# A spectral-filter and SwiGLU block on one core: Strassen products for one more chunk, with the scaling of w_down by gb moved to GpSimd

## The chip, the cores and the metric

The kernel runs on one core of a Trainium2 chip. The metric is the device time of one execution in microseconds (us). In a fast run the time lies within 1.5% of the kernel's fastest. A ratio is the mean time of one kernel's fast runs over the mean of the other's from the same rounds, with a 95% interval, so it is not quite the ratio of the medians that are quoted beside it. Below 0.98 counts as faster, above 1.02 as slower.

Engine names in the profile: PE is TensorE (matmul), PEld its weight loads, DVE is VectorE, ACT is ScalarE, POOL is GpSimd.

## The reference

```python
mod = (silu(c) @ w_mod).reshape(1, 6, 1, -1)           # sa, ca, ga, sb, cb, gb
h = layernorm(x) * (1 + ca) + sa                       # x: 2048 x 640, bf16
x = x + ga * irfft2(rfft2(h) * (w_r + 1j * w_i))       # spectral filter
h = layernorm(x) * (1 + cb) + sb
x = x + gb * ((silu(h @ w_gate) * (h @ w_up)) @ w_down)   # 640 -> 1728 -> 640
```

The change touches the last two lines, and the end of the third, with which they overlap.

## The kernel before

The 2048 rows are 16 tiles of 128. The last step of the spectral filter, called **phase 3** here, makes one tile after the other: TensorE multiplies, VectorE adds the residual from PSUM. Meanwhile the second layer norm of the first tiles starts: squares on ScalarE, variance on VectorE, the power -1/2 on GpSimd, normalization on VectorE, a transposing DMA, and the modulation (1 + cb, sb) in place, which is called "mod" below.

The feed-forward part then runs in five chunks of 2, 4, 4, 4 and 2 tiles. Each chunk has a gate/up stage (called C0 to C4) and a down stage (D0 to D4). In C0 and C1 gate/up is plain: 5 products for each of the 26 outputs. From C2 on it is a Strassen form: 7 block products in place of 8, for which sums of weight blocks (`GS`, `UG`) are needed once. The kernel before makes those sums in C1 on VectorE. It also scales the 14 row blocks of w_down by gb (`wd_fold`) on VectorE, five in phase 3 and nine in C0.

```python
def ln2_mod(ci):
    h2T = h2T_of(ci)
    for c5 in range(NC5):
        if ci == 0:
            nc.gpsimd.tensor_scalar(h2T[:, :, c5, :], h2T[:, :, c5, :], one_p_cb[:, c5:c5 + 1], modcols[:, 2, c5:c5 + 1],
                                    ALU.mult, ALU.add)
        elif c5 % 2 == 0 or ci > 1:
            nc.vector.tensor_scalar(...)          # the same operands
        else:
            nc.scalar.activation(...)
...
def gu_table(i, q):                                # weight sums, 256 columns at a time
    fs = slice(256 * q, 256 * q + 256)
    tt = nc.vector.tensor_tensor
    up1, up2, ga1, ga2 = (gu_w(u, k)[:, :, fs] for u in (1, 0) for k in range(2))
    s1, s2, s3, s4 = (g[:, :, fs] for g in GS)
    if i == 0:
        tt(s1, ga1, ga2, ALU.add)
    elif i == 1:
        tt(s2, s1, up1, ALU.subtract)
    elif i == 2:
        tt(s3, up1, ga1, ALU.subtract)
    elif i == 3:
        tt(s4, up2, s2, ALU.subtract)
    else:
        tt(UG[:, fs], Wgu[:, 1, 4, fs], Wgu[:, 0, 4, fs], ALU.subtract)

def wd_fold(f2):
    nc.vector.tensor_tensor(Wd_sb[:, f2, :], Wd_sb[:, f2, :], gb_bc[:], ALU.mult)
...
for t in range(NT):                                # phase 3
    ...                                            # six matmuls into PSUM
    nc.vector.scalar_tensor_tensor(x1[:, t, :]..., ops..., 1.0, x_sb[:, t, :]..., ALU.mult, ALU.add, accum_out=st2[:, t, 0:1])
    ...
    if 4 <= t <= 5:
        ln2_xn(0, t - 4)                           # normalization
    if t == 5:
        ln2_tr(0)                                  # transposing DMA
        load_gu(1024, 1664)
    ...
    if t == 10:
        ln2_mod(0)
    if t >= 7 and t % 2:
        wd_fold((13, 0, 1, 2, 3)[(t - 7) // 2])
...
for ci, (t0, n) in enumerate(chunks):
    if ci >= 2:
        gate_up_pairs(ci, ATc)                     # Strassen
    else:
        for fc in range(NFC - 1):                  # 13 column blocks
            half(0)                                # 5 matmuls, Silu on ScalarE
            half(1)                                # 5 matmuls, product on VectorE
            if ci == 0:
                if fc < 9:
                    wd_fold(fc + 4)
                ...                                # squares, variance; ln2_xn for chunk 1
                if fc == 10:
                    wd_rest()                      # copies of w_down's last row block
            else:
                for q in (2 * fc, 2 * fc + 1):
                    if q < 24:
                        gu_table(q % 4, q // 4)
                if fc % 2 == 1:
                    gu_table(4, fc // 2)
                ...
```

## Time and profile before

| | before |
|---|---|
| median of 3 runs | 259.76 us (258.53 to 259.96) |
| profiled span, mean granted clock | 258.0 us, 0.992 |
| TensorE, VectorE, ScalarE, GpSimd busy | 96%, 78%, 58%, 27% |

From the chain of waits of the kernel before, in order of time: start, length, engine and line, number of instructions.

```profile
87.62 14.19 PE psum L1015 x130
...
110.44 28.06 PE psum L1015 x130
```

L1015 is the plain gate/up, first C0, then C1. With the five matmuls at 109.36 that the fence leaves out, C1 takes 109.36 to 138.50, 29.14 us, and C2, in the Strassen form with as many tiles, follows the same chain from 152.24 to about 179, 26.8 us. That difference is what the change wants.

The same kernel by windows (from : to, length, busy time with number of instructions of PE, PEld, DVE, ACT and POOL, granted clock, DMA share, GB/s), one for C0, one for C1, one for C2:

```profile
87.10:101.80 14.70, 14.70 (x137) 12.99 (x137) 13.72 (x42) 8.14 (x23) 2.02 (x2) 1.00 0.25 49
109.40:138.50 29.10, 29.10 (x137) 13.07 (x135) 25.94 (x66) 15.59 (x31) 1.32 (x1) 1.00 0.02 6
152.20:179.00 26.80, 26.80 (x234) 22.41 (x231) 20.21 (x46) 18.30 (x34) 0.00 (x0) 1.00 0.06 17
```

TensorE has no gap in any of them. In C0 VectorE is busy for 13.72 of 14.70 us.

GpSimd in the kernel before, from its timeline (start, length, line, operation, out and in with shapes, count, idle time before it):

```profile
81.08 3.24 POOL L767 TENSOR_SCALAR rW<-rW,one_p_cb,modcols 128x256 bf16<-128x256 bf16 x5 [5.51 <-DMA rW<-rL]
90.72 1.01 POOL L741 TENSOR_TENSOR rstd_1286<-rstd_1286,mhalf 128x4 f32<-128x4 f32 x1 [6.40 <-DVE rstd_1286 L737]
```

Around the end of phase 3 GpSimd does five mods for chunk 0 (L767) and a variance power (L741), and little else. It looks free. While it does the mods, VectorE does two folds, in 0.49 and 0.57 us; the other folds take 0.48 or 0.49.

### The profile page before, as it was taken

The numbers are of one execution on the slowest core, as the hardware profiler recorded it, in microseconds if no ns is written. First come the engines' busy times: TensorE is split into PE (matmuls) and PEld (weight loads), VectorE is DVE, ScalarE is ACT, GpSimd is POOL, SyncE is SP. The second block draws the span as 40 slices with busy tenths as digits, with TensorE's granted clock in tenths as the row PEclk, the third lists the DMA queues.
The fourth block names the chain that finished last, engine by engine and source line by source line (L and its number), as shares of the span: only waits on it lengthen the run. The fifth ranks groups of instructions, "written<-read, shape, count | busy, mean of one in ns | idle before, by whom it ended". The sixth has DMA issues, their size and how long they took to land.

```text
span 258.0 us, 6291 instructions
## 1 busy us (share of the span) xinstructions
PE 248.6 (96%) x2423; PEld 191.8 (74%) x2423; DVE 202.3 (78%) x529; ACT 150.9 (58%) x280; POOL 69.3 (27%) x121
## 2 busy tenths in 40 slices
PE   7999997999999999999999999999999999999994
PEld 3778866899789888744445678886678887669963
DVE  2599788998889897499886966788875878875682
ACT  3578756998678664028652367765256676225740
POOL 4277772577214011000020450000450000440012
PEclk9799999999999999999999999999999999999999
DMA  7989999999998205100003211000412000211001
GB/s 233 392 249 303 290 404 198 174 387 381 316 307 211 102 5 104 41 14 9 0 3 71 70 42 36 3 0 12 94 51 64 0 0 4 51 53 56 3 3 51
DMA packets 44923, 30.84 MB, mean 120 GB/s; under 512 B 21599, under 2 KB 43102, under 8 KB 44510
## 3 DMA queue, kind: packets, MB, share of 16 engines
q1 hardware_dynamic: 44748, 30.23, 40.8%
q8 instruction: 19, 0.31, 0.5%
q10 hardware_dynamic: 146, 0.21, 0.3%
q14 instruction: 10, 0.08, 0.1%
HBM read 22.87 MB, written 4.72 MB: 107 GB/s over the span
## 4 chain that ended last, share of the span: by engine, by line
PE 74%; DVE 5%; ACT 2%; issue 2%; POOL 1%; POOLq 0%; ACTq 0%; DVEq 0%
PE psum L1041 22%; PE psum L1015 18%; PE psum L928 16%; PE psum L913 3%; PE psum L649 3%; PE psum L586 2%; PE psum L550 2%; PE psum L812 2%; PE psum L994 2%; PE psum L815 2%; DVE rM L573 1%; PE psum L607 1%; PE psum L638 1%; PE psum L654 1%; ACT rE L622 1%
## 5 line engine op out<-in xcount | busy, mean ns | idle before, releaser
L1015 PE MATMUL psum<-rW 128*128 128x512 bf16 (+1 forms) x290 | 49.0, 328 | 0.0
L1015 PEld LDWEIGHTS <-rW 128*128 128x128 bf16 x290 | 28.3, 98 | 18.4
L1041 PEld LDWEIGHTS <-rW 128*128 128x128 bf16 (+1 forms) x396 | 34.1, 98 | 3.6
L1041 PE MATMUL psum<-rW 128*128 128x256 bf16 (+1 forms) x252 | 35.3, 255 | 0.0
L953 POOL TENSOR_TENSOR rM<-rM,rL 128x320 f32<-128x320 f32 x7 | 7.8, 1117 | 100.5 <-ACT rL L949 100.5
L928 PEld LDWEIGHTS <-rX 128*128 128x128 bf16 (+1 forms) x175 | 15.8, 97 | 8.8 <-issue 1.8
L573 DVE TENSOR_TENSOR rM<-psum,rW 128x384 bf16<-128x384 f32 (+2 forms) x42 | 20.5, 542 | 1.4 <-PE psum L550 1.1
L928 PEld LDWEIGHTS <-rE 128*128 128x128 f16 x168 | 16.4, 98 | 6.9 <-DVE rE L885 0.6
L899 DVE TENSOR_TENSOR rA<-psum,rM 128x320 bf16<-128x320 f32 x25 | 11.6, 484 | 12.0 <-POOL rM L957 5.8
L928 PE MATMUL psum<-rE 128*128 128x320 f16 x126 | 20.6, 299 | 0.3 <-DVE rE L885 0.3
L1018 ACT ACTIVATE rX<-psum 128x256 f32<-128x256 f32 (+1 forms) x26 | 12.7, 487 | 13.0 <-PE psum L1015 12.2
L1041 PE MATMUL psum<-rE,rW 128*128 128x256 f16 (+1 forms) x144 | 19.9, 255 | 0.0
L928 PE MATMUL psum<-rA,rX 128*128 128x320 bf16 (+1 forms) x119 | 19.5, 301 | 0.1
L741 POOL TENSOR_TENSOR rstd_1286<-rstd_1286,mhalf 128x4 f32<-128x4 f32 (+2 forms) x4 | 4.0, 1010 | 51.4 <-DVE rstd_1286 L737 51.4
L1021 DVE TENSOR_TENSOR rX<-psum,rX 128x256 bf16<-128x256 f32 (+1 forms) x26 | 14.4, 557 | 2.6 <-PE psum L1015 2.3
L389 DVE SCALAR_TENSOR_TENSOR rE<-rE,mv,psum 128x648 bf16<-128x648 f32 (+1 forms) x17 | 14.1, 841 | 2.4 <-PE psum L322 2.1
L342 ACT COPY rE<-psum 128x640 bf16<-128x640 bf16 x16 | 11.1, 691 | 6.7 <-PE psum L340 6.7
L817 DVE SCALAR_TENSOR_TENSOR rM<-psum,rX 128x640 f32<-128x640 f32 x16 | 13.1, 821 | 2.1 <-PE psum L815 2.1
L1091 DVE TENSOR_TENSOR rX<-rH,rL 128x512 bf16<-128x512 bf16 x15 | 6.4, 425 | 10.3 <-ACT rL L1089 10.3
L589 ACT CAST rY<-psum 128x512 bf16<-128x512 f32 (+2 forms) x21 | 12.2, 589 | 3.8 <-PE psum L586 3.7
L1041 PEld LDWEIGHTS <-rE 128*128 128x128 f16 x144 | 12.7, 98 | 1.5
L657 ACT CAST rL<-psum 128x640 bf16<-128x640 f32 x16 | 10.9, 689 | 4.0 <-PE psum L654 3.0
(198 smaller groups left out, 622.0 us busy)
## 6 DMA issues: line engine op xcount, KB each, us to landing
out_dram<-rA SPq DMA_DIRECT2D x32, 80.0 KB, 1.6
rM<-in_w_mod_dram SPq DMA_DIRECT2D x3, 800.0 KB, 9.4
rA<-in_B_w_down_dram SPq DMA_DIRECT2D x1, 2080.0 KB, 17.3
rX<-in_A_x_dram SPq DMA_DIRECT2D x3, 640.0 KB, 9.6
rM<-in_w_mod_dram SPq DMA_DIRECT2D x1, 1600.0 KB, 7.4
rW<-in_B_w_gate_dram SPq DMA_DIRECT2D x2, 640.0 KB, 7.0
rW<-in_B_w_up_dram SPq DMA_DIRECT2D x2, 640.0 KB, 8.2
rW<-in_A_w_i_dram SPq DMA_DIRECT2D x1, 1024.0 KB, 11.0
```

The costliest lines, as they stand in the source:

```text
L342: nc.scalar.copy(hT[:, :, 0:128], _rev(xt, 127, [[128, NC5], [-1, 128]]) if flipped(t) else xt)
L389: nc.vector.scalar_tensor_tensor(Zv[:, h], Cv[:, h], mv[:, t, 0:1], zps[:, h], ALU.mult, ALU.subtract)
L573: nc.vector.tensor_tensor(PP[:, 1:4, hl], xv[:, :, hl], in1, ALU.mult)
L589: nc.scalar.copy(Y2[:, 0:n, :], yps[:, 0:n, :])
L657: nc.scalar.copy(VT[:], vps[:, 0:5, :])
L817: nc.vector.scalar_tensor_tensor(x1[:, t, :].rearrange("p (m r) -> p m r", r=4), ops.rearrange("p r m -> p m r"), 1.0, x_sb[:, t, :].rearr ...
L899: nc.vector.tensor_tensor(xo, src, x1[:, t, lo:lo + 320], ALU.add)
L928: nc.tensor.matmul(o, lhsT=lhsT, rhs=rhs, start=start, stop=stop, skip_group_check=True)
L1015: nc.tensor.matmul(gu[u], lhsT=Wgu[:, u, c5, ff * 128:(ff + 1) * 128], rhs=h2T[:, :, c5, :], start=(c5 == 0), stop=(c5 == NC5 - 1))
L1018: nc.scalar.activation(sg[:, 0:N], gu[0], ACT.Silu)
L1021: nc.vector.tensor_tensor(ATc[:, ff, :], gu[1], sg[:, 0:N], ALU.mult)
L1041: nc.tensor.matmul(o[:, f], lhsT=w, rhs=b, start=(start and f == 0 and i == 0), stop=(stop and f == F - 1 and i == len(ops) - 1), skip_gro ...
```

## The change

Its intent: run C1 in the Strassen form as well. The weight sums must then exist before C1, so they move into C0. To make room on VectorE, the 14 folds go to GpSimd, the first sum (S1) is made by two DMAs that GpSimd issues (one converts gate's upper half to fp16, the second adds the lower half), chunk 1's normalization goes to ScalarE, and the mods for chunk 0 go from GpSimd to VectorE, one a tile.

```diff
-    def ln2_mod(ci):
+    def ln2_mod(ci, cs=range(NC5)):
-        for c5 in range(NC5):
-            if ci == 0:
-                nc.gpsimd.tensor_scalar(...)
-            elif c5 % 2 == 0 or ci > 1:
+        for c5 in cs:
+            if c5 % 2 == 0 or ci != 1:
                 nc.vector.tensor_scalar(...)
@@
     def gu_table(i, q):
-        fs = slice(256 * q, 256 * q + 256)
+        fs = slice(512 * q, 512 * q + 512)
@@
     def wd_fold(f2):
-        nc.vector.tensor_tensor(Wd_sb[:, f2, :], Wd_sb[:, f2, :], gb_bc[:], ALU.mult)
+        nc.gpsimd.tensor_tensor(Wd_sb[:, f2, :], Wd_sb[:, f2, :], gb_bc[:], ALU.mult)
+    def gu_dma(k):
+        w = B_w_gate[256 * k:256 * k + 256, 0:1536].rearrange("(c5 dp) f -> dp c5 f", dp=P)
+        nc.gpsimd.dma_start(GS[0][:], w, accum_op=ALU.add if k else ALU.bypass)
@@ before phase 3
+        gu_dma(0)
@@ phase 3, after tile t
+            if t == 8:
+                gu_dma(1)
-            if t == 10:
-                ln2_mod(0)
-            if t >= 7 and t % 2:
-                wd_fold((13, 0, 1, 2, 3)[(t - 7) // 2])
+            if 10 <= t <= 14:
+                ln2_mod(0, (t - 10,))
+            if t == 14:
+                ln2_var(2, 4)
+                ln2_pow(2, 4)
+            for q in range(max(t - 4, 0), min(t - 3, 9)) if t < 14 else range(9, 14) if t == 15 else ():
+                wd_fold((13, 0, 6, 1, 7, 2, 8, 3, 9, 4, 10, 5, 11, 12)[q])
@@ chunks
-        if ci >= 2:
-            gate_up_pairs(ci, ATc)
+        if ci:
+            gate_up_pairs(ci, ATc, [...normalization of chunk 2 and five wd_tables... if ci == 1 else []])
         else:
+            tables = [lambda i=i, q=q: gu_table(i, q) for q in range(3) for i in range(1, 5)]
             for fc in range(NFC - 1):
@@
-                    if fc < 9:
-                        wd_fold(fc + 4)
-                    if 3 <= fc <= 6:
-                        ln2_xn(1, fc - 3)
+                for _ in range(2 if fc < 8 else 1):
+                    if tables:
+                        tables.pop(0)()
+                if 1 <= fc <= 4:
+                    ln2_xn_act(1, fc - 1)
... (squares rearranged; chunk 1's input sums made in D0, five of the eight down tables moved
     from D0 to C1; the last tiles' variance and power moved from C1 to the start of D1;
     the whole plain form of chunk 1 removed)
```

Nine folds stand in phase 3 on GpSimd, five more behind the power that C1's normalization needs.

More of the change, by code (lines that the diff above doesn't have):

```diff
@@ L761, in ln2_tr @@
             xn2c[:, 0:n].rearrange("p tl (c q) -> p (tl c) q", c=NC5))
-    def ln2_mod(ci):
+    def ln2_mod(ci, cs=range(NC5)):
         h2T = h2T_of(ci)
-        for c5 in range(NC5):
-            if ci == 0:
-                nc.gpsimd.tensor_scalar(h2T[:, :, c5, :], h2T[:, :, c5, :], one_p_cb[:, c5:c5 + 1], modcols[:, 2, c5:c5 + 1],
-                                        ALU.mult, ALU.add)
-            elif c5 % 2 == 0 or ci > 1:
+        for c5 in cs:
+            if c5 % 2 == 0 or ci != 1:
                 nc.vector.tensor_scalar(h2T[:, :, c5, :], h2T[:, :, c5, :], one_p_cb[:, c5:c5 + 1], modcols[:, 2, c5:c5 + 1],
@@ L917, in down_plain @@
                 ln2_mod(1)
-        for i in range(4):
+                h_sums(1)
+        for i in range(3):
             wd_tables(i, 0)
-            wd_tables(i, 1)
     def down_pair(ATc, t, j, nxt):
@@ L1022, in gu_plain, with gate_up_pairs @@
         return half
-    def gate_up_pairs(ci, ATc):
+    def gate_up_pairs(ci, ATc, extra):
         n = chunks[ci][1]
@@ L1110, in gate_up_pairs @@
             step(7, p - 2)
+            if p and extra:
+                extra.pop(0)()
             if n == 2:
@@ L1149, in adaln_block_kernel @@
         ATc = AT[:, 0:NFC * N].rearrange("p (f q) -> p f q", f=NFC)
-        if ci >= 2:
-            gate_up_pairs(ci, ATc)
+        if ci:
+            gate_up_pairs(ci, ATc, [lambda i=i: (ln2_xn_act(2, i), wd_tables(i, 1)) for i in range(4)] + [lambda: wd_tables(3, 0)] if ci == 1 else [])
         else:
             fin13 = gu13(ci, ATc)
+            tables = [lambda i=i, q=q: gu_table(i, q) for q in range(3) for i in range(1, 5)]
             for fc in range(NFC - 1):
@@ L1160, in adaln_block_kernel @@
                     fin13()
-                if ci == 0:
-                    if fc < 9:
-                        wd_fold(fc + 4)
-                    if fc in (0, 2, 4, 6):
-                        ln2_sq(6 + fc // 2)
-                    if fc == 0:
-                        ln2_var(2, 4)
-                        ln2_pow(2, 4)
-                    if 3 <= fc <= 6:
-                        ln2_xn(1, fc - 3)
-                    if fc == 6:
-                        ln2_tr(1)
-                    if fc == 8:
-                        ln2_var(6, 4)
-                        ln2_pow(6, 4)
-                    if fc == 10:
-                        ln2_nb(6, 4)
-                        wd_rest()
-                else:
-                    for q in (2 * fc, 2 * fc + 1):
-                        if q < 24:
-                            gu_table(q % 4, q // 4)
-                    if fc % 2 == 1:
-                        gu_table(4, fc // 2)
-                    if fc in (4, 8, 12):
-                        for i in range(4):
-                            a_sum(ATc, 0, i, slice(fc // 2 - 2, fc // 2))
-                    if fc < 6:
-                        ln2_sq(10 + fc)
-                    if fc == 7:
-                        ln2_var(10, 6)
-                        ln2_pow(10, 6)
-                    if fc == 10:
-                        ln2_nb(10, 6)
-                    if 6 <= fc <= 9:
-                        ln2_xn_act(2, fc - 6)
+                if fc == 0:
+                    ln2_nb(2, 4)
+                if fc == 8:
+                    ln2_var(6, 4)
+                    ln2_pow(6, 4)
+                if fc == 10:
+                    ln2_nb(6, 4)
+                    wd_rest()
+                for _ in range(2 if fc < 8 else 1):
[3 more added lines that the diff above has]
+                    ln2_xn_act(1, fc - 1)
+                if fc == 4:
+                    ln2_tr(1)
+                if fc in (0, 5, 6, 7, 8, 9, 10, 12):
+                    ln2_sq({0: 6}.get(fc, fc + 2 if fc < 12 else 13))
+            ln2_sq(14)
+            ln2_sq(15)
         if ci == 0:
@@ L1200, in adaln_block_kernel @@
         if ci == 1:
-            a_sum(ATc, 0, 4)
+            ln2_var(10, 6)
+            ln2_pow(10, 6)
+            ln2_nb(10, 6)
         if ci + 1 < len(chunks):
```

## The prediction

> **What bounds it.** TensorE: the page gives it 96% of a 258.0 us span, and the chain of waits is 74% TensorE matmuls, almost unbroken from the first gate/up (87.1 us) to 243 us. By stretch of that chain: chunk 1 (four tiles, plain gate/up) takes 109.36 to 138.50 = 29.14 us; chunks 2 and 3 (four tiles, Strassen) take 26.81 us each. The clock is 0.99.
>
> **What changes.** Chunk 1 gets the Strassen form: 216 half-width products instead of 120 full ones. The 30 weight sums that VectorE made inside chunk 1 (0.42 us each, six small ones 0.29) move into chunk 0 (two tiles, 14.2 us of products). To make room there:
> - the 14 w_down folds (0.49 us each on VectorE, nine in chunk 0) go to GpSimd;
> - the first sum comes from a casting DMA and an accumulating DMA, 0.79 MB each, issued by GpSimd;
> - chunk 1's normalization goes to ScalarE (0.91 us x4), with six more squares (0.92 us each) in chunk 0.
>
> **Costs, estimated.** TensorE: 29.14 - 26.81 = **2.33 us saved**, all on the chain. So about 257.4 us is the floor.
> VectorE in chunk 0: nine 1024-wide sums at 0.70 us (estimate from 0.42 at 512 and 0.65 at 960) and three at 0.42: 7.6 us in place of nine folds and four normalizations (6.9 us). It was 93% busy there and stays full.
> ScalarE: about 15.5 us for 14.7 us of window, so its last gates come 0 to 1 us late.
> GpSimd: a 128x320 f32 two-input op took 0.86 us undisturbed; a 640-wide bf16 fold should take 1.0 us (if bytes count) to 1.5 us (if elements count). The Trainium skill (GPSIMD Engine Reference, § 3.1) says about 2.6 cycles per element for two inputs; 0.86 us agrees. Folds start near 76 us, when the row-13 weights land. The variance power for chunk 1 stands behind nine folds and a DMA issue: ready at 88 to 91.5 us. VectorE wants it at 89.7 us. Five folds remain.
> Contention: the Trainium skill (SBUF — State Buffer, § Who interferes with whom) says a VectorE op with two SBUF inputs and a reading GpSimd op exclude each other. The trace agrees: in the down stage at 142 to 145 us VectorE sums grew from 0.56 to 1.0-1.2 us beside GpSimd adds. Five late folds can cost VectorE 0 to 5 us; the PSUM ring absorbs about four column blocks (4.4 us).
>
> Net: 2.33 us saved, less 0.5 to 1 us (late gates, chunk 1's fuller ScalarE and VectorE), less 0 to 6 us of chunk 0 stall, most likely about 0.5.
>
> **Prediction: 259.0 us, 80% within 257.2 to 264.5.** Faster by over 2%: 0.02; within 2%: 0.84; slower by over 2%: 0.14.
>
> **What would show it.** Chunk 1's gate/up near 26.8 us by the chain. Chunk 0's gate/up longer than 14.7 us, TensorE waiting there for VectorE products or for ScalarE gates; VectorE waiting for the GpSimd power or the accumulating DMA; VectorE sums of 1 us or more beside folds; GpSimd folds of 1.0 to 1.5 us.
>
> **What would make it wrong.** Folds at 1.5 us or above with exclusion: chunk 0 loses 5 to 8 us and the change is a loss. An accumulating DMA landing after 92 us does the same. If folds end before 88 us, nothing stalls and it is 257.5. A late transposition for chunk 0, behind the new DMA traffic, would stall phase 3.

## More of the kernel before

From the profile page of the kernel before: busy time in us, share of the span and instructions of each engine, then the rows of three engines in 40 equal slices of the span (6.45 us each), each digit a busy share in tenths (9 is 90% or more).

```profile
PE 248.6 (96%) x2423; PEld 191.8 (74%) x2423; DVE 202.3 (78%) x529; ACT 150.9 (58%) x280; POOL 69.3 (27%) x121
...
PE   7999997999999999999999999999999999999994
...
DVE  2599788998889897499886966788875878875682
...
POOL 4277772577214011000020450000450000440012
```

TensorE is full nearly everywhere. VectorE is at 8 or 9 tenths from the sixth slice to the fifteenth; phase 3 lies in slices 11 to 14, C0 in slices 14 to 16.

## The result

| | before | after |
|---|---|---|
| median | 259.53 us (258.53 to 259.96, 4 runs) | 270.06 us (269.38 to 270.80, 4 runs) |
| ratio, 95% | | 1.0412 (1.0369 to 1.0455): slower |
| profiled span, clock | 258.0 us, 0.992 | 268.0 us, 0.987 |

The change costs 4%. A table by stage tells where. Each number is the time from the first TensorE matmul of a stage to the first of the next, read from TensorE's timeline; "start" is the time before phase 3.

| stage | before | after | difference |
|---|---|---|---|
| start | 69.27 | 67.97 | -1.30 |
| phase 3 | 17.64 | 24.80 | **+7.16** |
| C0 | 14.83 | 20.51 | **+5.68** |
| D0 | 7.45 | 7.45 | 0 |
| C1 | 29.23 | 27.12 | **-2.11** |
| C2 | 26.91 | 27.31 | +0.40 |
| C4 and D4 | 24.83 | 24.99 | +0.16 |

D1 to D3 and C3 agree to 0.01 us. The sum is +10.0 us, as the spans differ. The start is not the change's doing: the window from 8 to 16 us of the profile before has a granted clock of 0.79, that of the profile after has 1.00, and the code there is the same.

So the gain is there, and of the size that was predicted. It is lost more than six times over before it begins. The profile page after, the same three rows of slices (6.7 us each):

```profile
PE   8999988999985686999999999999999999999994
...
DVE  2898789999799899867899798678895678884682
...
POOL 4487733776099193100000450000342000241002
```

TensorE's hole lies in slices 13 to 16 (80 to 107 us), and GpSimd is full in slices 12, 13 and 15. The chain of waits of the kernel after goes through VectorE there:

```profile
82.22 6.12 DVE rW L767
88.34 0.75 DVE rM L819 x2
```

L767 is the mod, L819 VectorE's residual sum from PSUM in phase 3. In C0 the same chain goes through two of the weight sums. VectorE's timeline of the kernel after has the same operations with shapes (start, length, line, operation, out and in, count):

```profile
82.13 6.20 DVE L767 TENSOR_SCALAR rW<-rW,one_p_cb,modcols 128x256 bf16<-128x256 bf16 x1
...
89.00 0.34 DVE L767 TENSOR_SCALAR rW<-rW,one_p_cb,modcols 128x256 bf16<-128x256 bf16 x1
...
96.34 1.96 DVE L788 TENSOR_TENSOR rE<-rY,rW 128x1024 f16<-128x1024 f16 x1
98.23 1.88 DVE L790 TENSOR_TENSOR rW<-rW 128x1024 f16<-128x1024 bf16 x1
...
100.37 1.55 DVE L792 TENSOR_TENSOR rE<-rW,rE 128x1024 f16<-128x1024 bf16 x1
101.84 1.61 DVE L794 TENSOR_TENSOR rH<-rW 128x512 f16<-128x512 bf16 x1
```

The first mod took 6.20 us, the next 0.34 us. The first four weight sums took 1.96, 1.88, 1.55 and 1.61 us; in the second and third round of the same sums the first three took 0.68 and the last, 512 wide, 0.41. GpSimd's timeline of the kernel after for the same stretch (L797 the folds, L801 the second DMA's issue, L741 the power):

```profile
74.28 5.97 POOL L797 TENSOR_TENSOR rA<-rA,gb_bc 128x640 bf16<-128x640 bf16 x4
80.18 1.24 POOL L801 DMA_DIRECT2D rY<-in_B_w_gate_dram  x1
81.02 7.22 POOL L797 TENSOR_TENSOR rA<-rA,gb_bc 128x640 bf16<-128x640 bf16 x5
93.99 1.04 POOL L741 TENSOR_TENSOR rstd_1286<-rstd_1286,mhalf 128x4 f32<-128x4 f32 x1 [5.75 <-DVE rstd_1286 L737]
95.01 8.15 POOL L797 TENSOR_TENSOR rA<-rA,gb_bc 128x640 bf16<-128x640 bf16 x5
```

The first mod ended at 88.33 and the run of five folds at 88.24, to within a tenth of a microsecond. The four slow weight sums (96.34 to 103.45) lie inside the other run of five folds (95.01 to 103.16), but for the last 0.3 us. What TensorE made of it is seen in its timeline, with the idle time before each piece and what ended it in brackets:

```profile
89.13 0.43 PE L814 MATMUL psum<-rH,rL 128*128 128x320 bf16 x1 [4.90 <-DVE rM L819]
...
100.50 1.25 PE L1022 MATMUL psum<-rW 128*128 128x256 bf16 x10 [0.81 <-DVE rX L1028]
103.83 1.25 PE L1022 MATMUL psum<-rW 128*128 128x256 bf16 x10 [2.08 <-DVE rX L1028]
105.57 4.61 PE L1022 MATMUL psum<-rW 128*128 128x256 bf16 x26 [0.49 <-DVE rX L1028]
```

TensorE stood for 4.90 us in phase 3, then for 0.81, 2.08 and 0.49 us in C0. The rest of the loss is TensorE's own speed. In windows of one microsecond (columns as above):

```profile
90.00:91.00 1.00, 1.00 (x11) 1.00 (x10) 0.94 (x4) 0.00 (x0) 0.00 (x0) 0.50 0.17 39
91.00:92.00 1.00, 1.00 (x9) 0.84 (x8) 0.49 (x3) 0.54 (x1) 0.00 (x0) 0.58 0.02 9
92.00:93.00 1.00, 1.00 (x12) 0.73 (x11) 0.73 (x1) 0.15 (x1) 0.00 (x0) 1.00 0.00 0
```

The windows just before have 0.71 and 0.50: TensorE goes on at half clock from 89.1 to about 91.6. The same happens after the gaps in C0: the granted clock is 0.74, 0.50, 0.50 and 0.55 in the four microseconds from 105 on. Lost clock times busy time, summed over these windows, is about 1.4 us for phase 3 and 1.6 us for C0. The Trainium skill (TensorE: Matmul & The Clock Gate, Part 1) says that the clock falls to half after an idle window of about 3.4 us and recovers after about as long a busy one. Phase 3 agrees roughly: 4.9 us of idle, then 2.5 us at half. In C0 no single gap is as long (2.08 us), yet the clock fell after three gaps within six microseconds (99.7 to 105.6); there the measurement decides.

### The profile page after: what moved, and what is told of

Same layout as the page of the kernel before. It is cut to its first block, busy times and chain, and to the rows that moved or that the text cites. A ratio compares the mean times of both kernels' runs of the same rounds, so it can differ in the third digit from the quotient of the medians.

```text
span 268.0 us, 6514 instructions
## 1 busy us (share of the span) xinstructions
PE 249.8 (93%) x2519; PEld 202.2 (75%) x2519; DVE 216.0 (81%) x521; ACT 163.0 (61%) x302; POOL 88.6 (33%) x132
## 4 chain that ended last, share of the span: by engine, by line
PE 64%; DVE 11%; issue 5%; ACT 3%; POOL 2%; POOLq 0%; DVEq 0%; ACTq 0%
PE psum L1048 28%; PE psum L935 15%; PE psum L1022 8%; PE psum L920 3%; PE psum L586 2%; DVE rW L767 2%; PE psum L550 2%; DVE rM L819 1%; DVE rA L906 1%; PE psum L607 1%; PE psum L1001 1%; PE psum L814 1%; PE psum L817 1%; POOL rE L633 1%; PE psum L649 1%
## 5 line engine op out<-in xcount | busy, mean ns | idle before, releaser
L1048 PEld LDWEIGHTS <-rW 128*128 128x128 bf16 (+1 forms) x528 | 47.0, 98 | 6.0 <-issue 0.6
L1048 PE MATMUL psum<-rW 128*128 128x256 bf16 (+1 forms) x336 | 48.9, 259 | 0.0
L1022 PE MATMUL psum<-rW 128*128 128x256 bf16 (+1 forms) x170 | 25.3, 305 | 3.4 <-DVE rX L1028 3.4
L1048 PE MATMUL psum<-rE,rW 128*128 128x256 f16 (+1 forms) x192 | 27.7, 259 | 0.3 <-ACT rH L1080 0.2
L1022 PEld LDWEIGHTS <-rW 128*128 128x128 bf16 x170 | 17.4, 103 | 8.7 <-issue 4.1
L741 POOL TENSOR_TENSOR rstd_1286<-rstd_1286,mhalf 128x4 f32<-128x4 f32 (+2 forms) x4 | 4.1, 1024 | 59.2 <-DVE rstd_1286 L737 59.2
L935 PEld LDWEIGHTS <-rE 128*128 128x128 f16 x168 | 16.4, 98 | 6.9 <-DVE rE L892 0.6
L797 POOL TENSOR_TENSOR rA<-rA,gb_bc 128x640 bf16<-128x640 bf16 x14 | 21.3, 1676 | 0.0
L1048 PEld LDWEIGHTS <-rE 128*128 128x128 f16 x192 | 17.4, 98 | 2.3
L1074 ACT COPY rW<-psum 128x512 f32<-128x512 f32 x21 | 12.3, 587 | 9.4 <-PE psum L1048 9.3
L1088 DVE TENSOR_TENSOR rX<-psum,rX 128x512 f32<-128x512 f32 x21 | 14.5, 689 | 3.7 <-ACT rX L1087 3.4
L1087 ACT COPY rX<-psum 128x512 f32<-128x512 f32 x21 | 12.3, 587 | 7.7 <-PE psum L1048 7.6
L1084 DVE TENSOR_TENSOR rH<-psum,rW 128x512 bf16<-128x512 f32 x21 | 14.5, 690 | 2.0 <-PE psum L1048 0.6
```

The lines of the kernel that those rows point to most:

```text
L797: nc.gpsimd.tensor_tensor(Wd_sb[:, f2, :], Wd_sb[:, f2, :], gb_bc[:], ALU.mult)
L935: nc.tensor.matmul(o, lhsT=lhsT, rhs=rhs, start=start, stop=stop, skip_group_check=True)
L1022: nc.tensor.matmul(gu[u], lhsT=Wgu[:, u, c5, ff * 128:(ff + 1) * 128], rhs=h2T[:, :, c5, :], start=(c5 == 0), stop=(c5 == NC5 - 1))
L1048: nc.tensor.matmul(o[:, f], lhsT=w, rhs=b, start=(start and f == 0 and i == 0), stop=(stop and f == F - 1 and i == len(ops) - 1), skip_gro ...
L1074: nc.scalar.copy(c0, X)
L1084: nc.vector.tensor_tensor(c11, Z, c0, ALU.add)
```

## The experiments

Theory A: GpSimd's folds and VectorE's operations exclude each other at a shared SBUF port. The Trainium skill (SBUF — State Buffer, § Who interferes with whom) says so of a VectorE instruction with two SBUF inputs beside a GpSimd instruction that reads SBUF, and says that a `tensor_scalar` which is not in the form with an accumulator output can contend too. A1, its refinement: the second DMA's issue, between the folds, puts GpSimd's cores out of step, so that neighbouring folds overlap and leave VectorE no moment to take the port. A2: VectorE loses the port to any long run of folds, with or without the DMA. Rival B: the mod waits for data, because the new DMA traffic delays the transposition; the folds are innocent. The ten runs below are each beside the kernel before on the same chip (medians 258.5 to 259.7 us there). The runs k1 to k6 have two executions each, r1 to r5 six. Every edit is against the changed kernel unless it says otherwise.

### k1: no folds (wrong result)

```diff
-                wd_fold((13, 0, 6, 1, 7, 2, 8, 3, 9, 4, 10, 5, 11, 12)[q])
+                pass
```

> The changed kernel with the 14 w_down folds left out (wrong result on purpose); both GpSimd DMAs and everything else stay. Theory A (GpSimd folds shut VectorE out of their shared SBUF port): the first chunk-0 modulation on VectorE falls from 6.2 us to about 0.34 us, the 1024-wide sums in chunk 0 all take 0.68 us, phase 3 loses its 4.9 us TensorE gap, and the total is 258 to 260 us. Rival B (the accumulating DMA, or the transposition behind it, holds the modulation): the gap of about 5 us stays and the total is 263 us or more.

Measured: 261.9 us, ratio 1.0127 (1.0098 to 1.0157). Phase 3 22.55, C0 15.28, C1 27.12. C0 loses its stall: the sums are at 0.68 and 0.41. But phase 3 still has a gap of 4.21 us, and VectorE's timeline of this kernel names another cause:

```profile
85.89 0.35 DVE L767 TENSOR_SCALAR rW<-rW,one_p_cb,modcols 128x256 bf16<-128x256 bf16 x1 [4.97 <-DMA rW<-rL]
```

With no folds to wait behind, GpSimd issues the second DMA at 74.2 and not at 80.2 us. The transposition for chunk 0, issued at 76.2, then lands 9.7 us later; in the changed kernel no transposition takes more than 6.6. So a delay of rival B's kind exists in this kernel: taking the folds out moved a DMA in front of the transposition. That the one delays the other is the likely reading of the times; no run separates it further. In the changed kernel the transposition for chunk 0, issued at 77.69, landed 3.7 us later, at about 81.4, before the first mod began at 82.13: there its data were not what the mod waited for. The rearranged DMA makes k1 a bad measure of what the folds cost in phase 3, and a good one for C0.

### k2: no second DMA (wrong result)

```diff
-            if t == 8:
-                gu_dma(1)
```

> The changed kernel with only the second, accumulating DMA left out (wrong result on purpose). The second DMA is issued on GpSimd between fold 4 and fold 5; after it the records of neighbouring folds overlap[...], before it they hardly do. Rival B (DMA holds the modulation): modulation 0.34 us, no phase 3 gap, total about 264 us or less. Theory A1 (the DMA issue puts the GpSimd cores out of step, so that from then on there is no moment between folds at which VectorE can take the port): folds no longer overlap, the first modulation waits for one fold only (1 to 1.8 us), each later one during the folds too, phase 3 gap 1 to 2 us. Theory A2 (any run of folds without a pause holds off a VectorE operation of this form): the modulation takes 6 us or more, until the ninth fold ends, total about 270 us.

Measured: 265.12 us, ratio 1.0252 (1.0222 to 1.0282). Phase 3 19.12, C0 21.72. The nine folds run without a break for 12.75 us, and still the first mod took 0.91 us and the next three 0.69 or 0.70. So a long run of folds does not hold VectorE off by itself; A2 falls. By itself this fits rival B too, as it takes DMA traffic away. C0 is longer here than in the changed kernel (20.51), and so it is in k5 below: the late folds collide as before, and in both the granted clock then stays near 0.50 for about seven microseconds (from 99 to 106), in the changed kernel for less than four.

### k5: the DMA stays, and GpSimd is brought into step after it

```diff
             if t == 8:
                 gu_dma(1)
+                nc.gpsimd.memset(warm2[:, 0:1], 0.0)
+                nc.gpsimd.tensor_copy(warm2[:, 1:2], warm2[:, 0:1])
```

> The changed kernel with two tiny GpSimd operations after the issue of the second DMA, the second of which waits for the first to be complete on all of GpSimd, so that the next fold starts from a common point; right result, everything else as in the changed kernel. Theory A1 (cores out of step after the DMA issue): the folds stop overlapping, the first modulation takes 1 to 1.8 us instead of 6.2, phase 3 loses 3 to 4 us of its gap, total 265 to 267 us. Theory A2 and rival B: no difference, modulation about 6 us, total 270 us.

Measured: correct, 266.35 us, ratio 1.0300 (1.0247 to 1.0352). Phase 3 19.30, C0 21.94. GpSimd's timeline of this kernel (L802 the DMA, L825 and L826 the two tiny operations, L798 the folds), then VectorE's (L768 the mod):

```profile
81.42 1.23 POOL L802 DMA_DIRECT2D rY<-in_B_w_gate_dram  x1
82.22 0.55 POOL L825 MEMSET warm<- 128x1 f32 x1
82.83 0.18 POOL L826 COPY warm<-warm 128x1 f32<-128x1 f32 x1
82.99 6.82 POOL L798 TENSOR_TENSOR rA<-rA,gb_bc 128x640 bf16<-128x640 bf16 x5
```

```profile
83.36 1.10 DVE L768 TENSOR_SCALAR rW<-rW,one_p_cb,modcols 128x256 bf16<-128x256 bf16 x1
```

The copy reads what the memset wrote and starts 0.06 us after its end (82.83 against 82.77). The DMA is issued, five folds follow it as before, and the first mod took 1.10 us in place of 6.20, the next four 0.69 or 0.70. All folds of the changed kernel and then of this one in one line each: count, shortest, median and longest in ns, first and last start.

```profile
L797 POOL TENSOR_TENSOR rA<-rA,gb_bc x14: 1385/1804/1846, 74.3 to 101.3; 128x640 bf16<-128x640 bf16 x14
```

```profile
L798 POOL TENSOR_TENSOR rA<-rA,gb_bc x14: 1385/1389/1842, 75.5 to 97.8; 128x640 bf16<-128x640 bf16 x14
```

In the changed kernel the five folds behind the DMA are recorded with 1.80 to 1.84 us each, yet they start every 1.36 us: each begins nearly half a microsecond before the record of the one before it ends (82.39 against 82.86 for the first pair). In k5 they take 1.39 us each and overlap by 0.03 us. The Trainium skill (GPSIMD Engine Reference, § 2.1 Instruction dispatch) says that consecutive instructions are no barrier between GpSimd's cores: a core starts the next one when its own share is done. The overlap of records agrees. The overlap and the long wait came together with the DMA and went together with two tiny instructions after it, so the part of A1 that the records can show is shown. That it is cores out of step rather than something else in GpSimd is the reading of that page and was not seen directly.

### k4: the mod in the form with an accumulator

```diff
+            if ci == 0:
+                nc.vector.tensor_scalar(h2T[:, :, c5, :], h2T[:, :, c5, :], one_p_cb[:, c5:c5 + 1], modcols[:, 2, c5:c5 + 1],
+                                        ALU.mult, ALU.add, accum_out=st_junk[:, 0:1])
```

> The changed kernel with the five chunk-0 modulations in the form of tensor_scalar that also writes out an accumulator (the values may come out wrong; this does not matter here): same engine, place, operands and waits, but by the Trainium skill not a 2-port form. Theory A (port): the first modulation takes 0.3 to 0.5 us although the folds run, no 4.9 us gap in phase 3, total 264 to 266 us because the late folds still slow the sums in chunk 0. Rival B (waiting for a DMA): it still takes about 6 us, total 270 us.

(The page that this text means is the one named at the head of this section.)

Measured: correct, 264.73 us, ratio 1.0237 (1.0177 to 1.0297), which leaves open whether it counts as slower. Phase 3 18.94, C0 20.56. GpSimd's five folds and VectorE's mods of this kernel, from the two timelines:

```profile
81.00 7.24 POOL L801 TENSOR_TENSOR rA<-rA,gb_bc 128x640 bf16<-128x640 bf16 x5
```

```profile
82.12 0.54 DVE L768 TENSOR_SCALAR_CACHE_REDUCE rW<-rW,one_p_cb,modcols 128x256 bf16<-128x256 bf16 x1
```

The run of folds is the changed kernel's to 0.02 us, overlapping records included, and each of the five mods goes through it in 0.54 us, 0.20 us more than the other form takes undisturbed. The data were there. This settles the long wait: rival B falls for the changed kernel, the wait hangs on the form of the instruction, as theory A says of the shared port, and 5.9 of phase 3's 7.2 us hang on the form of one VectorE instruction. Most of the rest looks like the same collision with another operation: beside the first folds the two normalizations of chunk 0, on VectorE in the form without an accumulator, took 1.68 and 0.94 us in the changed kernel and in k4, and TensorE then stood for 0.67 (0.65 in k4) and 0.34 us; in the kernel before and in k1, which has no folds, they took 0.61 us each. C0 stays as slow as it was, so the two losses are separate.

### k6: the five late folds back on VectorE

```diff
-            for q in range(max(t - 4, 0), min(t - 3, 9)) if t < 14 else range(9, 14) if t == 15 else ():
+            for q in range(max(t - 4, 0), min(t - 3, 9)) if t < 14 else ():
@@ C0
+                if 6 <= fc < 11:
+                    wd_fold((4, 5, 10, 11, 12)[fc - 6], nc.vector)
```

> The changed kernel with one thing undone in chunk 0 only: the five late folds (rows 4, 5, 10, 11, 12) go back to VectorE, one each after column blocks 6 to 10, when the weight sums are made; the nine folds of phase 3 stay on GpSimd. If the collision of late folds with the weight sums is what lengthens chunk 0's gate/up from 14.8 to 20.5 us, all twelve sums take 0.68 (or 0.41) us and chunk 0 takes 15 to 16 us, while the phase 3 gap of 4.9 us stays: total 264 to 266 us. If instead chunk 0 is long because VectorE or ScalarE is simply overfull, chunk 0 stays above 18 us and the total above 268 us.

Measured: correct, 266.09 us, ratio 1.0282 (1.0231 to 1.0334). Phase 3 25.36, C0 15.60. VectorE's timeline of this kernel (a 1024-wide sum, then a fold):

```profile
104.72 0.69 DVE L792 TENSOR_TENSOR rE<-rW,rE 128x1024 f16<-128x1024 bf16 x1
...
105.99 0.49 DVE L797 TENSOR_TENSOR rA<-rA,gb_bc 128x640 bf16<-128x640 bf16 x1
```

Every weight sum is at 0.68 to 0.69 or 0.42 us and C0 loses 0.77 us in place of 5.68. So in C0 4.9 us came from the late folds on GpSimd, which take 1.39 to 1.85 us each there and 0.48 to 0.49 us on VectorE. Phase 3 is as bad as in the changed kernel, as it should be.

### r1 and r2: both collisions removed, with and without the DMAs

r1 joins k4 and k6, writes chunk 0's normalization in the accumulator form too, keeps eight folds on GpSimd, and puts the sums that do not need the DMAs first. r2 is r1 with S1 made by VectorE and no DMA from GpSimd.

```diff
 r1:
+    ...tensor_scalar(xn2c..., ALU.subtract, ALU.mult, accum_out=st_junk[:, 1:2])
+    ...tensor_scalar(h2T..., ALU.mult, ALU.add, accum_out=st_junk[:, 0:1])       # ci == 0
+                if 6 <= fc < 12:
+                    wd_fold((4, 5, 9, 10, 11, 12)[fc - 6], nc.vector)
-            tables = [... for q in range(3) for i in range(1, 5)]
+            tables = [... for q in range(3) for i in (2, 4, 1, 3)]
 r2, besides:
-        gu_dma(0)
-            if t == 8:
-                gu_dma(1)
+            tables = [... for q in range(3) for i in (2, 0, 1, 4, 3)]
```

> A version meant to beat both: Strassen in chunk 1 as in the change; eight folds on GpSimd in phase 3, the six others on VectorE after column blocks 6 to 11 of chunk 0; the VectorE normalization and modulation of chunk 0 in the accumulator form that does not use the shared port; the sums that do not need the DMA's first sum made first. If the port collisions were the whole loss: phase 3 about 17.7 us as before, chunk 0 gate/up 15 to 15.5 us, chunk 1 gate/up 27.1 us (29.2 before), total 256.5 to 258 us against 258.6 to 259.5 before, ratio 0.990 to 0.998. If the rest of the moved work (ScalarE, DMA) also costs, the ratio is 1.00 or above.

> The repaired version without the two GpSimd DMAs: the first weight sum is made by VectorE too (three more 1024-wide sums of 0.68 us, 2.0 us in all, in chunk 0). If VectorE has the room in chunk 0, it is as fast as the repaired version or 0.3 us faster (less DMA traffic); if VectorE is the limit of chunk 0, chunk 0 is 1 to 2 us longer and the accumulating DMA was worth its place.

Measured, five rounds each, both correct, both within the 2% that counts as the same: r1 259.50 us, ratio 1.0037 (1.0011 to 1.0063); r2 261.17 us, ratio 1.0097 (1.0064 to 1.0131). By stage, r1: phase 3 18.22, C0 15.53, D0 8.62, C1 27.12, C2 27.30. So no stall of the size of the two collisions is left, C1 has its gain, and yet the kernel is no faster than before. C0 and D0 are 1.87 us longer, with VectorE's late folds and products last in line: 2.11 us won, 1.87 lost next to it, 0.58 in phase 3, 0.39 in C2. The DMAs were worth their place: without them C0 and D0 take 1.24 us more.

### r3, r4, r5: the same work in other places

All three give chunk 0's mods back to GpSimd (as before the change), keep nine folds there in phase 3, and compute the last tiles' variance power inside C1, not at the start of D1 as the change does; C2 then has its old 26.91, so C2's 0.40 us in the changed kernel most likely came from that; no run changes it alone. They differ in where VectorE's work of C0 goes.

```diff
 r3:  wd_rest (copies of w_down's last row block): from C0 to the end of D0
 r4:  r3, and the last third of the weight sums from C0 to the end of D0,
      three down tables from there into C1
 r5:  r4, but in D0:
+                if tl == 0 and h == 0:
+                    wd_rest()
+                    gu_table(2, 2)
                 out_store(t0 + tl, pops[tl % 2][h], h)
+                if tl == 0 and h == 0:
+                    gu_table(4, 2)
+                    gu_table(1, 2)
             if tl == 0:
                 ln2_mod(1)
                 h_sums(1)
+                gu_table(3, 2)
-      (and the three down tables back to the end of D0, as in the changed kernel)
```

> Second repair. Against the first: three folds run on GpSimd before chunk 0's variance power instead of after it, the chunk-0 modulations go back to GpSimd as in the kernel before (0.65 us each there), so that GpSimd makes nine folds and VectorE five; chunk 0's small odd-row copies move into chunk 0's down stage; the variance of the last six tiles moves from the start of chunk 1's down stage into chunk 1. If VectorE's load in chunk 0 and the wait for the variance power were what was left: phase 3 17.7 to 18.1 us (18.2 in the first repair), chunk 0 gate/up 15.0 to 15.4 (15.5), its down stage 7.5 to 8.0 (8.6), chunk 1 27.1 to 27.3, chunk 2 26.9 to 27.0 (27.3): ratio to before 0.994 to 0.998. Ratio 1.00 or more if ScalarE, not VectorE, sets chunk 0.

> Third repair: as the second, and the last third of the weight sums (used first by chunk 1's third group) is made in chunk 0's down stage instead of its gate/up, the w_down sums that stood there go into chunk 1. VectorE loses 2.2 us of work in chunk 0's gate/up. If VectorE is still its limit: chunk 0 14.8 to 15.1 us, ratio 0.991 to 0.996; if chunk 1's fuller VectorE then stalls TensorE, chunk 1 is 27.5 us or more and the gain is lost.

> r4 with its stages' lesson applied: chunk 0's gate/up keeps only the first two thirds of the weight sums (r4: 14.83 us, no loss); the last third's sums and the copies of w_down's last row go into VectorE's gaps of chunk 0's down stage (r4 shows 1.76 and 1.27 us idle there before its first two output sums), and only three down tables (1.83 us), as in the changed kernel, stand before chunk 1's first casts; the variance power of the last six tiles stays inside chunk 1 as in r3 and r4. Theory 'the gain is real and only VectorE's room in chunk 0 and around chunk 1's start decides whether it is kept': phase 3 18.2, chunk 0 gate/up 14.8 to 14.9, its down stage 7.45 to 7.6, chunk 1 gate/up 27.1 to 27.3, chunk 2 26.9; ratio to the kernel before 0.993 to 0.998. Rival 'a stall of the same size reappears wherever the VectorE work is put, because its total is too much for the stretch from phase 3 to chunk 1': the stages' sum is again not under the sum of the kernel before, ratio 1.000 to 1.008.

Measured, five rounds each, all correct and within the 2% that counts as the same:

| | median | ratio, 95% | phase 3 | C0 | D0 | C1 | C2 |
|---|---|---|---|---|---|---|---|
| before (profile) | | | 17.64 | 14.83 | 7.45 | 29.23 | 26.91 |
| r1 | 259.50 | 1.0037 (1.0011 to 1.0063) | 18.22 | 15.53 | 8.62 | 27.12 | 27.30 |
| r3 | 260.65 | 1.0045 (1.0014 to 1.0075) | 18.21 | 15.58 | 7.89 | 28.15 | 26.91 |
| r4 | 261.37 | 1.0074 (1.0053 to 1.0095) | 18.21 | 14.83 | 7.45 | 30.06 | 26.91 |
| r5 | 258.58 | 0.9994 (0.9969 to 1.0019) | 18.21 | 14.83 | 7.45 | 27.41 | 26.91 |

r4 frees C0 and D0 wholly and pays for it in C1, by TensorE's timeline of r4:

```profile
115.26 0.60 PE L1055 MATMUL psum<-rE,rW 128*128 128x256 f16 x4 [1.51 <-ACT rH L1087]
...
134.64 0.38 PE L1055 MATMUL psum<-rW,rE 128*128 128x256 bf16 x2 [1.31 <-DVE rX L1095]
```

Its VectorE comes to C1 with sums still to do and stays behind in it. r5 spreads the same sums over idle stretches of VectorE that r4's timeline shows in D0 (1.76 and 1.27 us) and keeps nearly all of the gain: from phase 3's first matmul to the end it takes 187.6 us where the profile before takes 188.7. The stages came out as that theory expected (C1 0.1 us over its range), and the rival's rule, that a stall of the same size turns up wherever the work is put, does not hold for r5. The measured ratio shows no gain, though; its interval includes 1, and neither expected range holds it well. The granted clock differs: four of r5's six runs have a mean of 0.993 (spans 256.8 to 257.1) and two 0.999 and 1.000 (256.1 and 255.8); of the eleven runs of before beside them one has 0.992 (258.1) and ten 1.000 (256.5 to 257.5). At full clock r5 is thus shorter by some 0.8 us, or 0.3%. Whether the kernel causes the lower clock is open: only one of the six runs left a trace, and that one was granted the full clock. The two kept traces with a mean of 0.992 or 0.993 and no long gap of TensorE, those of the kernel before and of r4, have the low clock at 8 to 12 us (0.57), long before the changed code runs; if r5's four runs have it there too, the change is not its cause. No version tried beat the kernel before by a margin that the runs can show.

## Why the prediction was wrong

- **The gain was right.** Predicted 2.33 us off C1, measured 2.11.
- **The stall of C0 was mis-sized.** The step is "less 0 to 6 us of chunk 0 stall, most likely about 0.5". It measured 5.68 us. The prediction had the mechanism (exclusion between folds and two-input sums), the right range for a fold (1.0 to 1.5 us; 1.39 measured undisturbed, up to 1.85 beside VectorE's sums) and even the case ("Folds at 1.5 us or above with exclusion: chunk 0 loses 5 to 8 us"), and gave it too little weight. It relied on this: "the PSUM ring absorbs about four column blocks (4.4 us)". (The ring is the set of PSUM banks that TensorE fills in turn while VectorE empties them.) The ring did not cover it, because VectorE was 93% busy in C0 already: four sums that grew by 4.55 us together (1.96 + 1.88 + 1.55 + 1.61 in place of 3 x 0.68 + 0.41) left nothing to catch up with, and TensorE stood as soon as the ring was full, 0.81 + 2.08 + 0.49 us, and then ran at half clock for three microseconds. k6 and k1 show the size: 4.9 to 5.2 us of C0's loss go with the late folds.
- **Phase 3 had no term at all.** It measured +7.16 us, the larger half. With the C0 stall alone the sum would be about 263 us (259.5 - 2.1 + 5.7); the missing term makes 270 of it. The prediction counted only the five late folds as collisions, not the nine early ones, and it did not cost the mods' move from GpSimd to VectorE: 0.34 us each, in a form that folds hold off. Nor did it ask what the folds do to the normalizations of chunk 0, which were on VectorE already. k4 shows that 5.9 us hang on that form, k5 that the long wait (6.20 us in place of one fold's) hangs on the DMA issued between the folds.
- **ScalarE's lateness** ("its last gates come 0 to 1 us late") did not show as a cause of its own: TensorE's gaps in C0 all end on VectorE.
- **"A late transposition for chunk 0" did not happen** in the changed kernel. It happened in k1, where it cost 4.97 us of VectorE's waiting.
- **The DMA landed in time.** In the changed kernel no sum waited for it; in k4 the first sum waited 0.23 us. This part was right.
- **The power for chunk 1 came late**: predicted "ready at 88 to 91.5 us", it started at 93.99, because VectorE's variance stood behind the held mod. A consequence of the missing term.
- **"It was 93% busy there and stays full"** was right and was the main point, read too lightly. With both collisions removed (r1) the change still gains nothing: the sums that VectorE must make before C1, beside the folds, fill the stretch in which TensorE can least wait. The price of 2.1 us on TensorE is work on VectorE, and only where that work fits in real gaps do the stages keep most of the gain (r5), too little for the measured times to show.

## What to carry to other kernels

Before moving work to an idle engine, list which operations of the busy engine run at the same time and whether the two share a port; an operation of 0.34 us waited 6.20 us here. The form of the instruction decides: with an accumulator output the same mod took 0.54 us beside the same folds. And where TensorE's gain is bought with work on another engine, look first for the gaps on that engine's timeline: nearly the same work cost 1.9 us in C0 and D0 (r1), 2.9 us in C1 (r4) and 0.3 us when it was spread over gaps in D0 (r5).

## What the Trainium skill lacked or had wrong

- SBUF — State Buffer, § Who interferes with whom: it says that whoever issues first has the shared pair for the whole instruction. Nothing there tells that one VectorE instruction can be held off by a run of several GpSimd instructions: the mod waited through the changed kernel's five folds, 6.20 us for 0.34 us of work, and 1.10 us where GpSimd had been brought into step after its DMA (k5). What it says of the accumulator form agrees (0.54 us beside the same folds, k4), as it does of two-input sums (0.68 us alone, 1.55 to 1.96 us beside folds).
- GPSIMD Engine Reference, § 2.1 Instruction dispatch: it warns of cores that run ahead as a matter of stale data, not of time. Here the five folds behind a DMA issue overlapped by up to 0.48 us in the records and held VectorE off. A memset and a copy that waits for it, 0.55 and 0.18 us, ended that.
- GPSIMD Engine Reference, § 3.1 Elementwise — side-by-side cycle accounting: its 2.6 cycles per element for two inputs stands beside a measurement in fp32. At the 1.2 GHz of its own example, 640 elements make an estimated 1.39 us; the bf16 fold took 1.385 us at its shortest. So the bf16 fold ran at that rate, which the section does not say. The fp32 addition of 320 elements took 0.86 us undisturbed, where the same rate gives an estimated 0.69 us.
- DMA: Bandwidth & Descriptors says that an accumulating DMA must be issued from GpSimd, and has a fit of time against bytes for the DMAs issued from there, but no figure for accumulating or casting ones. The two DMAs here (768 KB each at the destination) landed 7.2 and 11.0 us after their issue, beside other transfers; the issue held GpSimd for 0.99 and 1.24 us.
- TensorE: Matmul & The Clock Gate, Part 1: one idle window of about 3.4 us is given as what halves the clock; further down the page says that frequent short idles do it too, without a length. In C0 of the changed kernel gaps of 0.81, 2.08 and 0.49 us within six microseconds were followed by a granted clock of 0.50.
